# Gram products from two 64x64 tiles of the key tile instead of block-diagonal key copies

## The chip, the cores and the metric

The kernel runs on one core of one Trainium2 chip. The metric is the device time of one execution in microseconds. The core has a matrix engine (PE, with its weight loads PEld listed apart), a vector engine (DVE), a scalar engine (ACT), a general engine (POOL), and a queue engine (SP) that issues most DMAs. Each engine takes its instructions strictly in the order in which the built program holds them; an instruction that waits holds up all behind it on its engine.

## The reference

The kernel computes a delta-rule attention of 4 batches, 8 heads, 768 tokens and 48 features, and feeds its output, 3072 rows of 384, to a mixture of 8 experts with top-1 routing.

```python
k_n = k / (np.linalg.norm(k, axis=-1, keepdims=True) + 1e-06)
for t in range(S):
    y[:, :, t] = np.einsum('bhd,bhde->bhe', q[:, :, t], state)
    v_old = np.einsum('bhde,bhd->bhe', state, kt)
    state = state + bt[:, :, :, None] * np.einsum('bhd,bhe->bhde', kt, vt - v_old)
...
logits = x @ w_gate + modality_bias[modality_id]
e_idx = np.argmax(logits, axis=1)
h = np.maximum(x[mask] @ w1[e], 0.0)
out[mask] = gate_w[mask, None] * (h @ w2[e])
```

## The kernel before, in words

The recurrence is cut into 12 chunks of 64 tokens. A **group step** i = 2c+g is chunk c of one of two pairs of batches; there are 24. A step holds 16 heads, as 8 pairs x = 4p+j. Its key and query tile has 112 partitions: the 48 features of head 4h+j stand in rows 64h to 64h+47 (h = 0, 1), and for each x there are 64 key columns (a = 0) and 64 query columns (a = 1). For chunks 0 and 1 that tile is kqr, else ke, in five buffers; the load (L98, on SP) of ke i+5 waits until gram i has read its buffer.

`gram(i)` (L100) makes, for each x, the products of the step's keys with its keys and queries. The two heads of a pair must not mix. So it copies the keys into KB, a tile of 112 x 8 x 128 whose other blocks stay zero (cleared once, L85 and L86, one buffer on DVE and one on POOL): L111 to L113, one copy of 48x512 for each h, both on ACT for steps 0 to 3, one on ACT and one on DVE for 4 to 15, both on DVE from 16. Then L124 makes 8 products, 112x128 weights from KB by 128 moving columns, into two PSUM tiles gp (p = 0, 1). ACT and DVE copy the results out: G and gd (or D), the parts for the inverses (L126, L127), and P (L142, or L143 on DVE from step 16). From every second step of sets 2 to 5, G and gd go to DRAM by DMA (GD, L140).

An **inverse** (`inverse_`, L154) is made for each set of four steps, six sets m = 0 to 5. Its matrix A is a transposed copy of D for m = 0, 1 (L165, on DVE), and is loaded from GD by SP for the others (L166). ACT takes the root of its diagonal (s0, L175, named s01 for set 1, s02 for set 2), DVE goes on to t0 (t01, t02; L176 to L182) and scales A (L192), then DVE and POOL eliminate row by row (L213, L214: tm_x and T on DVE, tm_y and T on POOL). Set 0 is inverted in blocks of 16 and transposed to W0 (L225 to L228); `join` (L240) makes blocks of 32 from these: products jo on PE (L247), ya on DVE (L249), products on PE (L253), copies (R64, RTB). For set 1, D1's lower rows are filled late by ACT from PG (L150, "D<-PG"), behind the last copy of gram 13.

The **recurrence step** then runs: level products (L326, L335), the state's products ks (L363), RHS on DVE (L365), z (L378), ZT on ACT, the state's update (L386), the output y (L394), its store to xd, and the router's products for that step's 128 rows (L463, L468). After step 17 the first part of the routing and then the experts (L690, L733) start.

A scheduler with a timing model of its own sets the order on each engine when the program is built; a few gates (`issue_after`) bind single instructions to others. So a change of one part can move others.

Of the kernel before, what the change touches and what calls it, by code (L numbers as in the profile page):

```python
# [10 lines left out]
F32=mybir.dt.float32; F32R=mybir.dt.float32r; I32=mybir.dt.int32; U32=mybir.dt.uint32  # L11
# [3 lines left out]
class C:  # L15
    fl=4; mw=1; wn=2; kqb=5; kbb=2; thr=9; g0=17; nh=4; LA=2; LA0=1; ge=14; ge1=16; lgk={0:11,1:15,2:17,3:17}; gg={(12,0):('jy',0),(12,1):('jr',0),(13,0):('y1',0),(13,1):('r',0)}; ga=1; i1l=1; gdq=1;  gw=0; ww=512; t2e='vector'; dq1=('scalar','scalar'); jn={1:((1,0),)}; pf=0; gs=0
    invat={3:0,7:1,11:2,15:3,19:4,23:5}
    pgk=12; pgb=2; pgr=3; pg_q='sync'; gdb=2; kqr=2; kvb=2; r64=2; rtb=1; rcb=3; rbb=1; abuf=2; xob=2
    kb_q='sync'; gdfix='vector'; gdv=4; tmem='vector'; ascale='vector'; rscale='vector'; rcopy='mask'; rm_e='gpsimd'; vq='gpsimd'; yev='scalar'; sv=()
    x_q='sync'; xa_q='sync'; kv_q='sync'; ld_q='sync'; inv_q='sync'; w_q='sync'  # L20
    ap=(0,1); rp=(0,1); ra={0:('scalar','vector'),1:('scalar','vector')}; rs=(0,); i0=16; kb1=('scalar','vector'); g1=1; yq=2; na=1; xgb=4; wlp=('a1','b0'); wlq=(0,1,2,3); hpa=0; hpb=1; wide=1; zte=('scalar','scalar'); zti=4; pC_=None; pcn=(); gpt=('mo','ks','mo','y'); gpn=16; wte='vector'; ls=0; sp1=12; ti='gpsimd'; gde='scalar'; gde0='vector'; e16='scalar'; rh0='scalar'; as0='gpsimd'; dq=('vector','vector'); k1=1; rtg='gp'; rl=-1; fk=0; fz=0; fy=0; fi=0
    cA=9; tB=22; gt_e='gpsimd'; lb_e='vector'; TA=512; SB=1; SC=2; SE=1; eo=0; hold=1
# [3 lines left out]
    invp=(); kbc=24; dkb=0  # L26
    la_e='vector'; rw=dict(reuse_waits='tile'); pC=0; pI=None; pL=None; pin=(0,); pln=(0,); kbp=4; kbe0=('scalar','scalar'); kbe=('vector','vector'); pml=range(0,16); sp0=1; r0=6; NR=10; kg=0; a0=1; wr=4; gl=16; SA=4; i1=60

NS=16; NE=8

def copy(nc,n,o,i):
    if n=="scalar": nc.scalar.copy(o,i)  # L32
    else: getattr(nc,n).tensor_copy(o,i)
# [4 lines left out]
class Attention:  # L38
    """Chunked delta rule. Group step i=2c+g: 64 tokens of chunk c of batches 2g+p, heads 4h+j; x=4p+j."""
    def __init__(s,ident,ctx,pctx,tc,kq,kv,bblk,mask,xd,pm):  # L40
# [36 lines left out]
    def early(s,ctx):  # L77
        nc,tc=s.nc,s.tc
        s.pe=ctx[0].enter_context(s.tc.tile_pool(name="ag",bufs=1))
        s.pi=ctx[1].enter_context(s.tc.tile_pool(name="ai",bufs=1,side="right"))  # L80
        wt=s.wt=s.pe.tile([128,512],F32,name="wt")
        getattr(nc,C.wte).memset(wt,0.0)
        wz=s.pm.tile([128,512],F32,name="wz",tag="mo",bufs=2)
        for r in range(C.wn): nc.tensor.matmul(wz[:,0:C.ww],wt[:,0:128],wt[:,0:C.ww],start=True,stop=True)
        s.KB=[s.pe.tile([112,8,128],F32,name=f"KB{g}") for g in range(C.kbb)]  # L85
        for g,t in enumerate(s.KB): (s.nc.vector,s.nc.gpsimd)[g%2].memset(t,0.0)  # L86

# [12 lines left out]
    def gram(s,i):  # L100
# [8 lines left out]
        s.fetch(i)  # L109
        pg=s.PG[c]; k=s.KE[i]; KB=s.KB[i%C.kbb]  # L110
        for h in range(2):  # L111
            b=64*h
            copy(nc,(C.kbe0 if i<C.kbp else C.kb1 if i<C.i0 else C.kbe)[h],KB[b:b+48,:,b:b+64],k[b:b+48,:,0])  # L113
        s.Pt[i]=P=pg[:,512*g:512*g+512].rearrange("q (x t) -> q x t",x=8)
# [3 lines left out]
        for p in range(2):  # L118
          with s.gate(s.PI.get(C.gg.get((i,p)))):
            tg=C.gpt[(2*i+p)%len(C.gpt)] if i<C.gpn else "mo"  # L120
            gp.append((s.pm if tg=="mo" else s.ps).tile([128,4,128],F32,name=f"gp{i}_{p}",tag=tg,bufs=2 if tg=="mo" else None))
            for j in range(4):
                x=4*p+j
                nc.tensor.matmul(gp[p][:,j,:],KB[:,x,:],k[:,x].rearrange("r a t -> r (a t)"),start=True,stop=True)  # L124
        for p in range(2):
# [28 lines left out]
    def inverse_(s,m):  # L154
# [29 lines left out]
        def sub(X,a0,a1,b0,b1):  # L184
            """rows a0..a1, columns b0..b1 of the blocks on the diagonal"""
            return bass.AP(tensor=X.tensor,offset=X.offset+32*a0+b0,ap=[list(X.ap[0]),[33*B,nk],[32,a1-a0],[1,b1-b0]])
# [53 lines left out]
    def join(s,m,a,b):  # L240
        """blocks of 16 to blocks of 32 for columns a..b of W, D their Gram matrices"""
        nc=s.nc; N=b-a
        K=s.D[m].rearrange("q i x t -> q (i x) t")[:,a:b]; W0,W1=(t[:,a:b] for t in s.W[m])
        lv=s.ps.tile([128,512],F32,name=f"jo{a}",tag="gp")
        y,r=(lv[:,256*k:256*k+16*N].rearrange("q (n t) -> q n t",n=N) for k in range(2))
        for n in range(N):
            for q in range(0,128,32): s.PI['jy',a]=nc.tensor.matmul(y[q:q+32,n],K[q:q+16,n],W1[q:q+16,n,0:16],start=True,stop=True)  # L247
        ya=s.pw.tile([128,16,16],F32,name=f"ya{a}",tag="ya",bufs=1)
        s.PI['ya',a]=nc.vector.scalar_tensor_tensor(ya[:,0:N],y,s.m16,s.Ic.to_broadcast([128,N,16]),ALU.mult,ALU.add)  # L249
        if a==0 and C.gw:  # L250
            with s.gate(s.PI['ya',0]): s.w1b()
        for n in range(N):
            for q in range(0,128,32): s.PI['jr',a]=nc.tensor.matmul(r[q:q+32,n],W0[q:q+32,n],ya[q:q+32,n],start=True,stop=True)  # L253
        copy(nc,C.e16,W1[:,:,0:16],r)
        nc.vector.transpose(W0,W1)

    def joined(s,c,g):
        """inverse blocks of group g (or both) of a chunk of set 0"""
        if c not in s.KV: s.load(c)
# [143 lines left out]
def prep(q,k,v,beta):  # L403
    f=lambda a: a.reshape(2,2,2,4,12,64,48)  # g p h j c t e
    Q,K,V=f(q),f(k),f(v)
    kq=np.zeros((12,112,2048),np.float32); w=kq.reshape(12,112,2,2,4,2,64) # c r g p j a t
    for h in range(2):
        for a,X in enumerate((K,Q)): w[:,64*h:64*h+48,:,:,:,a]=X[:,:,h].transpose(3,5,0,1,2,4)
    kv=np.empty((12,2,64,2,2,2,4,48),np.float32) # c r t g a (two of p,h,j) e: keys with rows of a head, values with rows of a batch
    kv[:,:,:,:,0]=K.transpose(4,2,5,0,1,3,6)  # L410
    kv[:,:,:,:,1]=V.transpose(4,1,5,0,2,3,6)
    B=beta.reshape(2,2,2,4,6,2,2,32) # g p h j m cc b s
    bb=B.transpose(4,6,5,1,0,3,2,7).reshape(6,128,32).copy() # b cc p g j h
    for m in C.ap: bb[m]=B[:,:,:,:,m].transpose(2,5,4,0,1,3,6).reshape(128,32) # h b cc g p j
    t=np.arange(128)%64; mask=(t[:,None]<np.arange(64)[None,:]).astype(np.float32)
    return dict(kq=kq,kv=kv.reshape(12,128,1536),bblk=bb,mask=mask)
# [4 lines left out]
class Router:  # L421
    """Top-1 routing. Token tile i holds the rows of group step i. Tokens get places in lists of
    expert-pure slots: stages of whole 512-token slots first, the rest in 256-token slots."""
    def __init__(s,tc,pc,wg,mod,bias,ident):
# [45 lines left out]
    def rank(s,t0,t1,pw,ps,tag):  # L470
        """gates, experts, ranks among the tokens of an expert and one-hot ranks mod 128, of tiles t0..t1"""
        nc=s.nc; V=nc.vector; n=t1-t0; u=f"_{t0}"
# [37 lines left out]
    def stage(s,u,size,cap,col,pw):  # L510
        """share slots of size tokens out among the experts: slot experts, shift of the ranks"""
        nc=s.nc; V=nc.vector; m=s.edge[size].shape[1]
# [17 lines left out]
    def experts(s,u,hi,n,sei,pw):  # L530
        """expert of each slot, number of slots"""
        V=s.nc.vector
        T=lambda sh_,nm,dt=F32: pw.tile(sh_,dt,name=nm+u,tag=nm,bufs=1)
        cm=T([128,n,8],"cm"); V.tensor_tensor(cm,hi.unsqueeze(1).to_broadcast([128,n,8]),s.iot[:,0:n].unsqueeze(2).to_broadcast([128,n,8]),ALU.is_le)
        se=T([128,n],"se"); V.tensor_reduce(se,cm,AX.X,ALU.add)
        V.tensor_scalar(sei[:,0:n],se,7.0,None,ALU.min)
        V.tensor_copy(sei[:,n:n+1],hi[:,7:8])

    def look(s,u,t,Y,k,pw):
        """the values Y[k,expert] of the tokens' experts"""  # L540
        V=s.nc.vector; n=t//2
# [7 lines left out]
    def lists(s,u,t,pi,NH,out,pw,ps,tag,k):  # L549
        """place -> token and gate; NH columns of 128 places"""  # L550
        nc=s.nc; V=nc.vector; G=getattr(nc,C.lb_e)
# [71 lines left out]
class Experts:  # L623
# [10 lines left out]
    def weights(s,u,T,sei,col,gidx,c0,x,env,n=0):  # L634
        """weights and tokens of a slot"""
        nc=s.nc; E=getattr(nc,C.w_q)
# [63 lines left out]
    def layer1t(s,S):  # L700
        """layer 1 of 128 tokens: they are the rows of the products, which are transposed afterwards"""
        nc=s.nc; u=S["u"]; env=S["env"]; xh,xl=S["xh"],S["xl"]; W1,W2=S["W"][1],S["W"][2]
# [156 lines left out]
```

## Time and profile before

| | us |
|---|---|
| runs of the kernel | 552.22, 549.54, 549.57; median 549.57 |
| span of the profiled execution | 550.4 |
| PE busy | 483.5 (88%) |
| DVE busy | 364.5 (66%) |
| ACT busy | 263.5 (48%) |
| POOL busy | 208.5 (38%) |
| mean DMA rate over the span | 147 GB/s |

The times come from runs without the profiler; the profiled execution is one of its own, and its rows add up to its span. In the rows that follow, "out<-in" names the tiles with the buffer numbers left out, "xN" is a count, and a bracket at the end is the idle time just before, with what ended it. Weight loads (PEld) run beside products (PE). A PE row of a float32 product counts two records for each product in the program.

### The profile page before, as it was taken

The page shows a single profiled execution, that of the slowest core. Times are in us where ns is not written, and L with a number is a line of the kernel's source. Part 1 is how long each engine was busy: PE and PEld are TensorE (multiplying, and loading weights), DVE is VectorE, ACT ScalarE, POOL GpSimd, SP SyncE. Part 2 cuts the span into 40 slices and gives each one's busy share as a digit, 9 for nine tenths or more (in the row PEclk, how much of TensorE's full clock was granted, in tenths as well). Part 3 has the DMA queues.
Part 4 walks back from the last instruction along what each step waited for, and adds up shares of the span by engine and source line. Part 5 has one row for each costly group of instructions (what it writes and reads, how often), then busy time and mean ns, then how long its engine had stood idle before and what let it go on. Part 6 is the DMA issues. An engine that isn't in the chain of part 4 may idle for free. (4 is left out here: it accounts for less than half of the span.)

```text
span 550.4 us, 14025 instructions
## 1 busy us (share of the span) xinstructions
PE 483.5 (88%) x5459; PEld 432.1 (79%) x5459; DVE 364.5 (66%) x877; ACT 263.5 (48%) x619; POOL 208.5 (38%) x350
## 2 busy tenths in 40 slices
PE   7876875897898897998889997799999999999992
PEld 5776865786687776787768896689889898899992
DVE  5999899998789689577474499435536233437850
ACT  6855631655766567476565403043424334216540
POOL 9863477065066263111142136242303437111110
PEclk9977796588899799798889998699999999999997
DMA  8979741233594975838864224233623524427720
GB/s 205 247 200 238 176 105 55 64 95 89 169 226 138 236 180 166 209 120 230 228 192 142 76 80 127 75 116 114 209 79 120 170 75 164 128 78 227 233 85 9
DMA packets 82716, 80.81 MB, mean 147 GB/s; under 512 B 50105, under 2 KB 73671, under 8 KB 81520
## 3 DMA queue, kind: packets, MB, share of 16 engines
q1 hardware_dynamic: 79440, 70.18, 46.8%
q0 software_dynamic: 3200, 9.64, 5.2%
q8 instruction: 45, 0.74, 0.6%
q14 instruction: 31, 0.25, 0.2%
HBM read 65.12 MB, written 14.88 MB: 145 GB/s over the span
## 5 line engine op out<-in xcount | busy, mean ns | idle before, releaser
L733 PE MATMUL opa<-w2ha,h 128*128 128x384 f32 x256 | 69.1, 339 | 0.3 <-DVE ooa L736 0.3
L213 DVE TENSOR_TENSOR tm_x<-T,A 128x108 f32<-128x108 f32 (+12 forms) x165 | 57.8, 352 | 5.4 <-DVE PG L143 0.7
L124 PE MATMUL gp<-ke,KB 112*128 112x128 f32 x320 | 53.1, 331 | 9.3 <-DVE PG L143 3.9
L214 DVE TENSOR_TENSOR T<-T,tm_x 128x108 f32<-128x108 f32 (+12 forms) x165 | 56.8, 346 | 4.5
L124 PEld LDWEIGHTS gp<-ke,KB 112*128 112x128 f32 x320 | 48.3, 238 | 12.3 <-issue 3.7
L693 DVE SCALAR_TENSOR_TENSOR h<-hpa,h 128x512 fp32r<-128x512 f32 x32 | 22.0, 689 | 42.4 <-ACT h L692 42.4
L733 PEld LDWEIGHTS opa<-w2ha,h 128*128 128x128 f32 x256 | 46.2, 188 | 1.4 <-DVE ooa L736 0.5
L733 PE MATMUL opa<-w2la,h 128*128 128x384 f32 x128 | 43.0, 336 | 0.0
L692 ACT ACTIVATE h<-hpa 128x512 fp32r<-128x512 f32 x32 | 19.1, 596 | 49.5 <-PE hpa L690 49.5
L690 PE MATMUL hpa<-x,w1ha 128*128 128x512 f32 x144 | 39.1, 408 | 0.0
L340 POOL TENSOR_TENSOR kvn<-kvn,RR 128x384 f32<-128x384 f32 x22 | 18.7, 868 | 50.7 <-DMA kvn<-in_kv_dram 28.3
L363 PE MATMUL ks<-Sbd,kqr 112*64 112x96 f32 x352 | 27.3, 274 | 8.7 <-DMA kqr<-in_kq_dram 4.8
L365 DVE TENSOR_TENSOR RHS<-kvn,ks 64x384 f32<-64x384 f32 x44 | 24.2, 551 | 15.8 <-POOL kvn L340 9.4
L214 POOL TENSOR_TENSOR T<-T,tm_y 128x18 f32<-128x18 f32 (+8 forms) x90 | 30.7, 342 | 6.6
L213 POOL TENSOR_TENSOR tm_y<-T,A 128x18 f32<-128x18 f32 (+8 forms) x90 | 30.5, 339 | 6.6
L690 PEld LDWEIGHTS hpa<-x,w1ha 128*128 128x128 f32 x144 | 27.3, 194 | 5.5
L32 ACT COPY ZT<-z 64x384 f32<-64x384 f32 x48 | 22.7, 473 | 17.2 <-PE z L378 16.6
L363 PEld LDWEIGHTS ks<-Sbd,kqr 112*64 112x64 f32 x352 | 20.9, 150 | 11.8 <-ACT Sbd L32 4.4
L32 ACT COPY Sbd<-Sps 48x192 f32<-48x192 f32 x88 | 27.5, 313 | 5.2 <-PE Sps L386 2.7
L737 POOL DMA_INDIRECT out_dram<-ooa,sidxa x16 | 17.1, 1071 | 32.6 <-DMA out_dram<-ooa,sidxa 13.1
L657 POOL DMA_INDIRECT xga<-xd,gidxa x16 | 17.9, 1117 | 30.5 <-PE xpa L659 17.4
L378 PE MATMUL z<-RHS,R 128*64 128x96 f32 x384 | 26.9, 296 | 1.6 <-ACT R L338 1.6
(346 smaller groups left out, 1173.7 us busy)
## 6 DMA issues: line engine op xcount, KB each, us to landing
kvn<-in_kv_dram SPq DMA_DIRECT2D x12, 768.0 KB, 8.0
ke<-in_kq_dram SPq DMA_DIRECT2D x20, 448.0 KB, 6.8
kqr<-in_kq_dram SPq DMA_DIRECT2D x10, 896.0 KB, 6.9
w1ra<-in_moe_w_dram SPq DMA_DIRECT2D x16, 384.0 KB, 4.0
w2ra<-in_moe_w_dram SPq DMA_DIRECT2D x16, 384.0 KB, 3.2
xd<-xo SPq DMA_DIRECT2D x24, 192.0 KB, 2.5
w1rc<-in_moe_w_dram SPq DMA_DIRECT2D x8, 384.0 KB, 3.6
w2rc<-in_moe_w_dram SPq DMA_DIRECT2D x8, 384.0 KB, 3.2
```

What stands on the lines that cost most here:

```text
L32: if n=="scalar": nc.scalar.copy(o,i)
L124: nc.tensor.matmul(gp[p][:,j,:],KB[:,x,:],k[:,x].rearrange("r a t -> r (a t)"),start=True,stop=True)
L213: yield I.tensor_tensor(o,y,z,ALU.mult)
L214: yield I.tensor_tensor(x,x,o,ALU.subtract)
L340: if c: E(C.vq).tensor_tensor(V,V,w,ALU.mult)
L363: nc.tensor.matmul(ks[64*p:64*p+64,:,j,:],KQ[:,4*p+j,0],hc(Sb[:,4*p+j,:]),start=True,stop=True)
L365: b=64*p; nc.vector.tensor_tensor(RH[b:b+64,:,48*p:48*p+48].rearrange("q (h j) c -> q h j c",h=2),VN[b:b+64],ks[b:b+64],ALU.subtract)
L378: s.PI['z',i]=nc.tensor.matmul(z[64*h:64*h+64,:,j,:],R[:,2*j+h,:],hc(RH[:,4*h+j,:]),start=True,stop=True)
L690: nc.tensor.matmul(hp[:,v,:],w[:,k,fs],x[:,k,0:T],start=(n==0),stop=(n==8)); n+=1
L692: nc.scalar.activation(hh,hp,AF.Relu)
L693: nc.vector.scalar_tensor_tensor(hl,hp,0.0,hh.bitcast(F32),ALU.max,ALU.subtract)
L733: mm=nc.tensor.matmul(op,h[:,f%nf,ts_],w[:,f%2,:],start=(n==0),stop=(n==23)); n+=1
```

## The change

The copies into KB, the tiles KB, their clearing and the constants that chose their engines are gone. Each product of a pair becomes two, one for each head: weights are the 64 key columns of that head's 48 rows in the key tile, the moving columns the same rows' 128, and the result goes to 64 of the 128 rows of gp. What gp holds is the same. Comments and docstrings are removed as well, so lines stand 3 lower from L113 on (L247 is L244, L165 is L162, and so on) and 2 lower between L86 and L113.

```diff
-        s.KB=[s.pe.tile([112,8,128],F32,name=f"KB{g}") for g in range(C.kbb)]
-        for g,t in enumerate(s.KB): (s.nc.vector,s.nc.gpsimd)[g%2].memset(t,0.0)
...
-        pg=s.PG[c]; k=s.KE[i]; KB=s.KB[i%C.kbb]
-        for h in range(2):
-            b=64*h
-            copy(nc,(C.kbe0 if i<C.kbp else C.kb1 if i<C.i0 else C.kbe)[h],KB[b:b+48,:,b:b+64],k[b:b+48,:,0])
+        pg=s.PG[c]; k=s.KE[i]
...
-                nc.tensor.matmul(gp[p][:,j,:],KB[:,x,:],k[:,x].rearrange("r a t -> r (a t)"),start=True,stop=True)
+                for h in range(2):
+                    b=64*h
+                    nc.tensor.matmul(gp[p][b:b+64,j,:],k[b:b+48,x,0],k[b:b+48,x].rearrange("r a t -> r (a t)"),start=True,stop=True)
```

The built program's order differs at several places. On PE, these are the rows before around jo0, the products of set 0's join (W0_1, D0 and W0_0 are set 0's tiles, gpI_p the products of gram I; the number behind the last underscore is the program's own):

```order
L124 MATMUL gp8_1_469<-ke8_460,KB0_112 128x128 x4
L124 MATMUL gp9_0_486<-ke9_482,KB1_113 128x128 x4
...
L124 MATMUL gp13_1_592<-ke13_583,KB1_113 128x128 x4
L124 MATMUL gp14_0_1088<-ke14_1084,KB0_112 128x128 x4
L124 MATMUL gp14_1_1093<-ke14_1084,KB0_112 128x128 x4
L247 MATMUL jo0_619<-W0_1_283,D0_117 32x16 x32
L124 MATMUL gp15_0_1110<-ke15_1106,KB1_113 128x128 x4
```

and now:

```order
L121 MATMUL gp8_0_506<-ke8_504 64x128 x8
L121 MATMUL gp8_1_515<-ke8_504 64x128 x4
L244 MATMUL jo0_699<-W0_1_303,D0_113 32x16 x32
L121 MATMUL gp8_1_515<-ke8_504 64x128 x4
L121 MATMUL gp9_0_534<-ke9_532 64x128 x8
L121 MATMUL gp9_1_543<-ke9_532 64x128 x2
L250 MATMUL jo0_699<-ya0_732,W0_0_302 32x16 x32
L121 MATMUL gp9_1_543<-ke9_532 64x128 x6
```

The join moved from behind gram 14 to the middle of gram 8, so grams 9 to 14 stand behind it.

On ACT, these rows stood before around s02, the root that needs the loaded A2 (ZT0 is the copy of the recurrence's step 0, PG7 and gd7 are gram 15's results):

```order
L175 ACTIVATE s01_703<-A1_698,eps_96 128x32
L126 COPY PG7_1082<-gp15_1_1115 128x128
L32 COPY gd7_1083<-gp15_1_1115 128x128
...
L338 COPY R640_342<-y10_876 32x8x32 x2
L32 COPY ZT0_348<-z0_1306 64x8x48 x2
L175 ACTIVATE s02_913<-A2_908,eps_96 128x32
L126 COPY PG8_1341<-gp17_0_1739 128x128
```

and now:

```order
L139 COPY PG7_1162<-gp14_1_1175 128x256
L172 ACTIVATE s01_783<-A1_778,eps_96 128x32
L172 ACTIVATE s02_993<-A2_988,eps_96 128x32
L123 COPY PG7_1162<-gp15_0_1194 128x128
L32 COPY gd7_1163<-gp15_0_1194 128x128
...
L32 COPY ZT0_380<-z0_1398 64x8x48 x2
```

s02 moved ahead of gram 15's copies and of ZT0. On SP the load of A2 moved ahead of the load of ke19, which it followed.

On DVE, these rows stood before around t02, which needs s02 (tm1_x and T1 are set 1's elimination):

```order
L213 TENSOR_TENSOR tm1_x10_720<-T1_699,A1_698 128x30
L214 TENSOR_TENSOR T1_699<-T1_699,tm1_x10_720 128x30
L213 TENSOR_TENSOR tm1_x20_726<-T1_699,A1_698 128x58
L176 RECIPROCAL t02_914<-s02_913 128x32
L214 TENSOR_TENSOR T1_699<-T1_699,tm1_x20_726 128x2x29
L143 TENSOR_TENSOR PG8_1341<-gp17_0_1739,um_100 128x256
```

and now:

```order
L162 STREAM_TRANSPOSE A1_778<-D1_308 128x1024
L173 RECIPROCAL t01_784<-s01_783 128x32
L174 TENSOR_TENSOR t01_784<-t01_784,A1_778 128x32
L175 TENSOR_TENSOR t01_784<-t01_784,s01_783 128x32
L173 RECIPROCAL t02_994<-s02_993 128x32
L176 TENSOR_SCALAR rr1_786<-t01_784 128x32
...
L189 TENSOR_TENSOR A1_778<-A1_778,t11_785 128x1024
```

t02 moved ahead of set 1's scaling and elimination. Further on, the inverses of sets 2 to 5 stand earlier among the recurrence's steps on DVE: of the 330 elimination instructions, 173 stood ahead of the RHS of step 8, and 270 stand there now.

More of the change, by code (lines that the diff above doesn't have):

```diff
@@ L15 @@
 class C:
-    fl=4; mw=1; wn=2; kqb=5; kbb=2; thr=9; g0=17; nh=4; LA=2; LA0=1; ge=14; ge1=16; lgk={0:11,1:15,2:17,3:17}; gg={(12,0):('jy',0),(12,1):('jr',0),(13,0):('y1',0),(13,1):('r',0)}; ga=1; i1l=1; gdq=1;  gw=0; ww=512; t2e='vector'; dq1=('scalar','scalar'); jn={1:((1,0),)}; pf=0; gs=0
+    fl=4; mw=1; wn=2; kqb=5; thr=9; g0=17; nh=4; LA=2; LA0=1; ge=14; ge1=16; lgk={0:11,1:15,2:17,3:17}; gg={(12,0):('jy',0),(12,1):('jr',0),(13,0):('y1',0),(13,1):('r',0)}; ga=1; i1l=1; gdq=1;  gw=0; ww=512; t2e='vector'; dq1=('scalar','scalar'); jn={1:((1,0),)}; pf=0; gs=0
     invat={3:0,7:1,11:2,15:3,19:4,23:5}
@@ L20 @@
     x_q='sync'; xa_q='sync'; kv_q='sync'; ld_q='sync'; inv_q='sync'; w_q='sync'
-    ap=(0,1); rp=(0,1); ra={0:('scalar','vector'),1:('scalar','vector')}; rs=(0,); i0=16; kb1=('scalar','vector'); g1=1; yq=2; na=1; xgb=4; wlp=('a1','b0'); wlq=(0,1,2,3); hpa=0; hpb=1; wide=1; zte=('scalar','scalar'); zti=4; pC_=None; pcn=(); gpt=('mo','ks','mo','y'); gpn=16; wte='vector'; ls=0; sp1=12; ti='gpsimd'; gde='scalar'; gde0='vector'; e16='scalar'; rh0='scalar'; as0='gpsimd'; dq=('vector','vector'); k1=1; rtg='gp'; rl=-1; fk=0; fz=0; fy=0; fi=0
+    ap=(0,1); rp=(0,1); ra={0:('scalar','vector'),1:('scalar','vector')}; rs=(0,); i0=16; g1=1; yq=2; na=1; xgb=4; wlp=('a1','b0'); wlq=(0,1,2,3); hpa=0; hpb=1; wide=1; zte=('scalar','scalar'); zti=4; pC_=None; pcn=(); gpt=('mo','ks','mo','y'); gpn=16; wte='vector'; ls=0; sp1=12; ti='gpsimd'; gde='scalar'; gde0='vector'; e16='scalar'; rh0='scalar'; as0='gpsimd'; dq=('vector','vector'); k1=1; rtg='gp'; rl=-1; fk=0; fz=0; fy=0; fi=0
     cA=9; tB=22; gt_e='gpsimd'; lb_e='vector'; TA=512; SB=1; SC=2; SE=1; eo=0; hold=1
@@ L26 @@
     invp=(); kbc=24; dkb=0
-    la_e='vector'; rw=dict(reuse_waits='tile'); pC=0; pI=None; pL=None; pin=(0,); pln=(0,); kbp=4; kbe0=('scalar','scalar'); kbe=('vector','vector'); pml=range(0,16); sp0=1; r0=6; NR=10; kg=0; a0=1; wr=4; gl=16; SA=4; i1=60
+    la_e='vector'; rw=dict(reuse_waits='tile'); pC=0; pI=None; pL=None; pin=(0,); pln=(0,); pml=range(0,16); sp0=1; r0=6; NR=10; kg=0; a0=1; wr=4; gl=16; SA=4; i1=60
 NS=16; NE=8
```

## The prediction

> **What bounds the kernel now.** First the page's 40 slices (13.76 us each, tenths of busy time), then stretches of 20 and 50 us with each engine's busy time.
>
> ```profile
> PE   7876875897898897998889997799999999999992
> DVE  5999899998789689577474499435536233437850
> DMA  8979741233594975838864224233623524427720
> ```
>
> ```profile
> 20.00:40.00 20.00, 16.23 (x119) 15.73 (x120) 18.89 (x35) 13.24 (x51) 15.96 (x23) 0.83 0.88 219
> 40.00:60.00 20.00, 14.76 (x211) 13.53 (x209) 19.14 (x38) 11.89 (x42) 7.23 (x11) 0.74 0.98 245
> ```
>
> ```profile
> 350.00:400.00 50.00, 50.00 (x245) 44.53 (x245) 21.05 (x38) 17.12 (x27) 13.88 (x12) 0.94 0.41 127
> 400.00:450.00 50.00, 49.75 (x254) 44.80 (x254) 20.20 (x30) 18.11 (x30) 13.37 (x11) 1.00 0.36 112
> ```
>
> The columns are the stretch, its length, busy PE, PEld, DVE, ACT and POOL, the PE clock, the DMA share and GB/s. The experts at the end are PE's alone (50.00 of 50). From 20 to 60 us DVE is the full engine (18.89 and 19.14 of 20), and so, over 40 to 60, are the DMA engines (0.98). So what changes in the expert stage is nothing, and the question is when the recurrence delivers its tokens. Steps 8 and 17 of it measure that.
>
> ```profile
> 164.16 0.55 PE L463 MATMUL rxt<-ident,xo 128*128 128x128 f32 x3
> 164.63 0.88 PE L378 MATMUL z<-RHS,R 128*64 128x96 f32 x16
> ...
> 170.66 0.55 PE L463 MATMUL rxt<-ident,xo 128*128 128x128 f32 x3
> ```
>
> ```profile
> 237.96 0.88 PE L378 MATMUL z<-RHS,R 128*64 128x96 f32 x16
> ```
>
> Columns: start, duration, line, tiles, count. Step 8's z starts at 164.63, step 17's at 237.96, after which the router and the first experts can start. A step in which PE runs back to back takes 6.50 us (164.16 to 170.66). Nine steps took 73.33, where nine of 6.50 are 58.5: 14.8 us went into waits for later inverses and loads. I take a shift of step 17 as a shift of the end, since the PE-bound experts follow it.
>
> **The change, part by part.** *The products themselves.* A step's 8 products of 112x128 weights become 16 of 48x64.
>
> ```profile
> L124 PE MATMUL gp<-ke,KB 112*128 112x128 f32 x320 | 53.1, 331 | 9.3 <-DVE PG L143 3.9 <-issue 2.7 <-ACT s L175 1.1
> L33 DVE COPY KB<-ke 48x512 f32<-48x512 f32 x28 | 15.5, 553 | 0.8 <-PE gp L124 0.3
> L32 ACT COPY KB<-ke 48x512 f32<-48x512 f32 x12 | 7.5, 621 | 0.2
> L32 ACT COPY KB<-kqr 48x512 f32<-48x512 f32 x8 | 4.9, 617 | 3.1 <-DVE Ic L62 2.7 <-DMA kqr<-in_kq_dram 0.3
> ```
>
> ```profile
> 38.28 2.02 PE L124 MATMUL gp<-ke,KB 112*128 112x128 f32 x16 [0.19 <-ACT PG L142]
> 41.05 2.02 PE L124 MATMUL gp<-ke,KB 112*128 112x128 f32 x16 [0.75 <-ACT PG L142]
> ...
> 49.28 1.05 PE L247 MATMUL jo<-W,D 16*32 16x16 f32 x64 [3.55 <-DVE W L225]
> ...
> 60.56 0.69 PE L335 MATMUL y<-R,ys 32*32 32x32 f32 x32 [0.86 <-ACT ys L330]
> ```
>
> Each product leaves two records, so a step has 16 in 2.02 us, or 126 ns for 128 columns. The new step has 32 records; the moving columns stay 128. If the two tiles of a head pair run beside each other, a step stays near 2.02; if they queue, it takes 32 x 126 ns = 4.03. No row shows 64x64 tiles on a diagonal. The nearest is L335, 32x32 tiles on several rows: 32 records of 32 columns in 0.69, where 126 ns scaled to 32 columns (31.5 ns) would queue to 1.01. They overlap, so I take 2.02, with 4.03 as the other end. The Trainium skill's "TensorEngine Tiling (Array Packing)", Gotcha 1, speaks against this: different row tiles cannot use one PSUM bank at the same time, and here both tiles write halves of one gp tile. By that rule the step would take the 4.03 us; the L335 row, whose tiles also share a bank, does not bear it out. That is rival C.
>
> *The copies.* Gone are 28 on DVE (15.5 us), 20 on ACT (12.4) and a clearing each on DVE and POOL. On DVE this lies in its full stretch, so taken alone it is time on the path. Twelve of the 28 stand in the order ahead of W's first transpose (L225), which ends set 0's inverse.
>
> ```profile
> 48.19 1.03 DVE L225 STREAM_TRANSPOSE W<-T 128x512 f32<-128x512 f32 x1
> ...
> 52.98 1.91 DVE L165 STREAM_TRANSPOSE A<-D 128x1024 f32<-128x1024 f32 x1
> ```
>
> ```profile
> L86 DVE MEMSET KB<- x1: 912/912/912, 2.7 to 2.7; 112x1024 f32 x1
> ```
>
> It ends at 49.22; less 12 x 0.553 and the 0.91 clearing, at about **41.7**. Nothing else ahead of it changes.
>
> *What the order makes of it.* On PE the products of the join, jo0 on W0, move from behind gram 14 into the middle of gram 8. PE is in order, so grams 8 to 15 now wait for 41.7, although gram 9 to 13 need only their keys; before, grams 10 and 11 ran at 38.28 and 41.05. A step comes every 2.77 us there (41.05 - 38.28); without the 0.62 us copy on ACT perhaps every 2.15. I take 2.4: gram 11, 3.5 steps after the join's first half, is done at 50.1; gram 13, 5.5 steps after it, at 54.9. Two things hang on that. ACT's late copies of D1 follow gram 13:
>
> ```profile
> 43.85 3.30 ACT L32 COPY D<-PG 32x256 f32<-32x256 f32 x8
> ```
>
> so D1 is whole at 54.9 + 3.3 = 58.2 instead of 47.15, and DVE's transpose of A1 behind it ends at 60.1 instead of 54.9. And the key loads: with five buffers, ke16 waits for gram 11, ke18 for gram 13, and the load of A2 stands on SP behind them.
>
> ```profile
> 38.16 0.32 SPq L98 DMA_DIRECT2D ke<-in_kq_dram  x1
> ...
> 45.24 0.43 SPq L296 DMA_DIRECT2D kqr<-in_kq_dram  x1
> ...
> 50.09 3.86 SPq L98 DMA_DIRECT2D ke<-in_kq_dram  x1
> 54.05 0.38 SPq L166 DMA_DIRECT2D A<-GD x1
> ```
>
> ```profile
> 39.70:54.40 14.70, 9.77 (x150) 9.00 (x152) 14.16 (x24) 8.80 (x31) 6.21 (x9) 0.83 0.98 250
> ```
>
> ```profile
> DMA to landing us min/median/max: 3.2/5.0/6.8
> ```
>
> Before, ke16 was issued at 38.16 and the queue came to 50.09, 11.9 us later, before the wait for ke19's buffer, which A2 now precedes. The DMA engines moved 250 GB/s at a share of 0.98 meanwhile, so the backlog sets this pace. From 50.1: A2 issued at 62.0 and, with the longest landing of A's loads (the last row, 6.8), landed at **68.8**. The ends: 54.9 + 2 for the writes of GD3 + 3.2 gives 60.1; the whole stretch of 14.7 started only at ke18's issue, and a median landing of 5.0 behind it, give 75.
>
> *What waits for A2.* Now ACT has s02, the root of A2's diagonal, ahead of gram 15's copies and of ZT0, without which no recurrence step ends; and DVE has t02 ahead of the whole elimination of A1, where before t02 stood behind its first two columns. So DVE stands from A1's transpose until A2 has landed, and cannot use that time for A1's elimination.
>
> *What DVE does afterwards.* Counting in the order: between t02 and the RHS of step 8 there were 141 elimination instructions (L213, L214) and are now 241, for sets 3 and 4 stand ahead of it; ten KB copies there are gone.
>
> ```profile
> 64.51 0.35 DVE L176 RECIPROCAL t<-s 128x32 f32<-128x32 f32 x1 [0.42 <-ACT s L175]
> ...
> 163.67 1.12 DVE L365 TENSOR_TENSOR RHS<-kvn,ks 64x384 f32<-64x384 f32 x2
> ```
>
> ```profile
> 64.00:165.00 101.00, 83.80 (x1575) 72.93 (x1576) 89.41 (x251) 53.04 (x151) 50.03 (x132) 0.82 0.43 112
> ```
>
> ```profile
> 64.00:165.00 101.00, 26.37 (x77) 0.82 0.43 112
> ```
>
> ```profile
> L192 DVE TENSOR_TENSOR A<-A,t x5: 1208/1218/1226, 60.8 to 183.2; 128x1024 f32<-128x1024 f32 x5
> ```
>
> The stretch from t02 to step 8 lasted 99.2 us with 89.4 busy. One elimination instruction takes 0.342 (the row with 26.37 is L213 alone, x77). New busy time: 89.4 + 100 x 0.342 - 10 x 0.553 + about 6 for the added sets' scalings (five as L192 at 1.22) = 124.1. Of the 9.8 idle I keep 4, since DVE now comes last more often. RHS of step 8: 69.3 (A2's 68.8 and the root) + 128.1 = **197.4**, its z 1 us later. In return all inverses are done early, and steps 8 to 17 can run at PE's 6.50: step 17's z at 198.4 + 58.5 = **256.9**, against 237.96: +18.9. Short: z17 = t02 + 187.6. The removal of the copies is in this sum; the reordering outweighs it.
>
> **Against the runs.** The profiled execution spans 550.4, the median of the runs is 549.57. 550.4 + 18.9 = 569.3 in the profile; 0.8 off for the runs, and 1.5 off because the wait of step 19 for its inverse goes as well: **567**.
>
> **Rivals.** A, *A2 is not late* (no change): the stall needs the DMA backlog. If grams 9 to 13 follow one another at 2.02 and A2 lands as soon as issued, t02 is not at 69 but near 52. By z17 = t02 + 187.6, no change is at t02 = 50.4; DVE's own work would let it reach t02 there (64.51 less 12 + 6 copies at 0.553 and the clearing is 53.6, and the first columns of A1 moved behind it). For: SP issues A2 one load earlier. Against: D1's copies alone hold A1 until 58.2. 549 to 553.
>
> B, *faster*: as A, and in addition the eliminations speed up, for one shape has two prices.
>
> ```profile
> 31.42 0.79 DVE L213 TENSOR_TENSOR tm_x<-T,A 128x110 f32<-128x110 f32 x1
> ...
> 40.98 0.27 DVE L213 TENSOR_TENSOR tm_x<-T,A 128x110 f32<-128x110 f32 x1
> ```
>
> If the mean of 0.342 fell to 0.29 with less beside them, 241 x 0.05 = 12 us would go: 537 to 546. It decides where t02 comes before 60. Against it: POOL's own eliminations, which run beside DVE's, stay.
>
> C, *the tiles queue*: 2.0 us more for each gram step. Steps 9 to 13 are ahead of A2: +10 on t02 at most, and steps 16 to 23 add PE time where it waits for DVE: 575 to 585.
>
> D, *that the copies' removal does nothing* (DVE hidden behind DMA) falls into A's times.
>
> **How the numbers follow.** Forecast (t02 60 to 75, z17 +9.6 to +24.6): 0.60; C 0.12; A and D 0.13; B 0.15. "Within 0.5%", about what a measurement of this kernel can tell from no change, is 2.7 us. Faster 0.15, same 0.13, slower 0.72. The forecast's own range is 557 to 573 and a little beyond for the idle kept (up to 5.8 more: 579). For 8 in 10 the range goes to 546 below, which takes in A, and to 581, part of C.
>
> **What would show it.** PE's idle time before L244 rises from 3.55 us to over 10 and ends on DVE's W. L121's steps of 32 records take near 2.0 us at full clock (4 would be C). A2's load is issued near 62, ACT's s02 waits for it, and DVE idles some 8 us or more before t02. Step 8's z lies near 198 and step 17's near 257, with 6.5 us between steps. The prediction is wrong if DVE does not idle before t02, or if the steps before 8 wait less for DVE than 124 us of work says.

## The result and the profile after

The changed kernel takes 586.45 us (583.08 to 587.92), the kernel before 549.57; the ratio is 1.0655, 95% interval 1.0607 to 1.0703. The profiled execution spans 586.1 us against 550.4. It is slower, as forecast, but by 36.9 us instead of 17.4, and outside the range (546 to 581).

The page's slices of the changed kernel, then its group of Gram products (count, busy us, mean ns of one, idle time before, and what ended it):

```profile
PE   8629567766849789899998999689999999999992
DVE  4981199999998569611378348934455423546750
PEclk9855865557856969999998899859999999999998
...
L121 PE MATMUL gp<-ke 48*64 48x128 f32 x640 | 61.5, 351 | 20.5 <-DVE PG L140 12.8
```

A slice is 14.65 us here. DVE is nearly idle in the fourth and fifth (44 to 73 us), where it had been full, and then full to about 190. The products of the 20 ke steps are busy for 61.5 us, where L124 had 53.1, and they wait 12.8 us for DVE's copies of P (L140), where it was 3.9. The rise in busy time isn't the price of the tiles: in e10 below, the same 640 records take 51.4.

The rows around the first inverse, PE's first, then SP's, then DVE's; a bracket is the idle time before a row:

```profile
40.08 1.05 PE L244 MATMUL jo<-W,D 16*32 16x16 f32 x64 [12.92 <-DVE W L222]
...
50.24 3.68 PE L121 MATMUL gp<-ke 48*64 48x128 f32 x32
```

```profile
65.91 3.91 SPq L163 DMA_DIRECT2D A<-GD  x1
```

```profile
65.10 1.95 DVE L162 STREAM_TRANSPOSE A<-D 128x1024 f32<-128x1024 f32 x1 [17.70 <-ACT D L32]
73.40 0.35 DVE L173 RECIPROCAL t<-s 128x32 f32<-128x32 f32 x1 [5.11 <-ACT s L172]
205.54 0.35 DVE L173 RECIPROCAL t<-s 128x32 f32<-128x32 f32 x1 [6.34 <-ACT s L172]
```

PE stands 12.92 us for W in the middle of gram 8. DVE then stands 17.70 us for D1's late copies and 5.11 for the root that needs A2. The third row is not in the prediction: at 205.54 DVE stands again, for set 5's root. Steps 8 and 17 of the recurrence, PE's row of z, and DVE's stretch that the prediction summed, from t02 to the RHS row that starts just ahead of step 8's z (216.71):

```profile
217.73 0.88 PE L375 MATMUL z<-RHS,R 128*64 128x96 f32 x16
```

```profile
278.82 0.88 PE L375 MATMUL z<-RHS,R 128*64 128x96 f32 x16
```

```profile
73.40:216.71 143.31, 102.80 (x1685) 87.59 (x1687) 122.46 (x352) 59.41 (x163) 66.54 (x168) 0.65 0.39 105
```

Step 17 comes 40.9 us later than before (237.96), the end 35.7. The stretch is 143.3 us with 122.5 busy on DVE, where it was 99.2 with 88.0 busy. (The prediction's 89.4 is of the 101 us from 64 to 165.)

One reading of the prediction has to be put right here. The row that it calls the RHS of step 8 (163.67 before) is that of step 9: steps 0 and 1 have no such row, and the one with 173 eliminations ahead of it, which is the count given for step 8, stands at 158.01. In the change the row with 270 ahead of it stands at 208.06, and 216.71 is step 9's. From t02 to step 8's own RHS the two kernels have, before first:

```profile
64.51:158.01 93.50, 76.53 (x1432) 66.52 (x1433) 82.83 (x235) 47.88 (x137) 43.78 (x115) 0.81 0.39 105
```

```profile
73.40:208.05 134.65, 95.22 (x1575) 80.91 (x1577) 118.29 (x338) 53.83 (x151) 61.55 (x156) 0.65 0.37 100
```

DVE is busy 118.3 us instead of 82.8, and idle 16.4 instead of 10.7. So the finding is the same by either row: the loss is mostly DVE's work, moved ahead of step 8.

### The profile page after: what moved, and what is told of

Read it like the earlier page. It is cut to its first block, busy times and chain, and to the rows that moved or that the text cites. A ratio compares the mean times of both kernels' runs of the same rounds, so it can differ in the third digit from the quotient of the medians.

```text
span 586.1 us, 14707 instructions
## 1 busy us (share of the span) xinstructions
PE 495.7 (85%) x5843; PEld 441.3 (75%) x5843; DVE 350.0 (60%) x848; ACT 253.0 (43%) x599; POOL 206.2 (35%) x349
## 4 chain that ended last, share of the span: by engine, by line
PE 56%; DVE 27%; DMA 6%; issue 4%; ACT 3%; SPq 1%; POOL 0%; POOLq 0%; ACTq 0%; DVEq 0%
PE hpa L687 12%; PE opa L730 10%; DVE T L211 7%; DVE tm_x L210 7%; PE gp L121 4%; PE hpc L687 3%; PE opc L730 3%; PE opb L730 3%; PE hpb L687 2%; PE Sps L465 2%; DMA A<-GD 2%; PE y L391 2%; PE Sps L383 2%; PE z L375 2%; DVE RHS L362 1%
## 5 line engine op out<-in xcount | busy, mean ns | idle before, releaser
L121 PE MATMUL gp<-ke 48*64 48x128 f32 x640 | 61.5, 351 | 20.5 <-DVE PG L140 12.8
L121 PEld LDWEIGHTS gp<-ke 48*64 48x64 f32 x640 | 52.8, 181 | 24.8 <-DVE PG L140 14.7
L210 DVE TENSOR_TENSOR tm_x<-T,A 128x108 f32<-128x108 f32 (+12 forms) x165 | 57.8, 352 | 6.1 <-issue 1.3
L211 DVE TENSOR_TENSOR T<-T,tm_x 128x108 f32<-128x108 f32 (+12 forms) x165 | 55.9, 340 | 4.9
L211 POOL TENSOR_TENSOR T<-T,tm_y 128x18 f32<-128x18 f32 (+8 forms) x90 | 32.2, 359 | 6.6
L123 ACT COPY PG<-gp 128x128 f32<-128x128 f32 x48 | 12.9, 268 | 44.2 <-PE gp L121 43.9
L210 POOL TENSOR_TENSOR tm_y<-T,A 128x18 f32<-128x18 f32 (+8 forms) x90 | 29.0, 323 | 6.8
L142 POOL TENSOR_SCALAR_AFFINE_SELECT PG<-PG 64x512 f32<-64x512 f32 x32 | 21.9, 686 | 16.0 <-ACT PG L139 14.7
L465 PE MATMUL Sps<-wg,rxs 128*128 128x96 f32 x144 | 25.0, 318 | 3.0 <-ACT rxs L462 3.0
```

The source lines that it names most:

```text
L121: nc.tensor.matmul(gp[p][b:b+64,j,:],k[b:b+48,x,0],k[b:b+48,x].rearrange("r a t -> r (a t)"),start=True,stop=True)
L142: for h in range(2): nc.gpsimd.affine_select(out=P[64*h:64*h+64],in_=P[64*h:64*h+64],compare_op=ALU.is_gt,fill=0.0,base=0,pattern=[[0,8],[ ...
L210: yield I.tensor_tensor(o,y,z,ALU.mult)
L211: yield I.tensor_tensor(x,x,o,ALU.subtract)
L465: for k in range(3): nc.tensor.matmul(s.lg[g][:,c0:c1,:],xs[:,k,:],s.wg[:,k,88-8*(c-c0):88+8*(c1-c)].rearrange("q (c e) -> q c e",e=8),sta ...
```

## The experiments

"Eliminations" are DVE's instructions of L213 and L214 (L210 and L211 in the change). Times of t02 and z are the starts in the profiled execution; the count ahead, of the RHS of steps 2 and 8, is that of the built order. Each ratio is to the kernel before, run on the same chip; the medians of different runs can be from different chips.

| run | join | ahead of step 2, 8 | t02 | z8 | z17 | median | ratio |
|---|---|---|---|---|---|---|---|
| before | behind gram 14 | 41, 173 | 64.5 | 164.6 | 238.0 | 549.57 | 1 |
| change | in gram 8 | 62, 270 | 73.4 | 217.7 | 278.8 | 586.45 | 1.0655 |
| e1 | in gram 8 | 59, 270 | 84.5 | 230.2 | 291.5 | 598.01 | 1.0842 |
| e2 | behind gram 13 | 83, 270 | 56.1 | 208.9 | 271.3 | 577.94 | 1.0478 |
| e3 | in gram 9 | 30, 174 | 77.2 | 174.2 | 247.1 | 554.28 | 1.0054 |
| e4 | behind gram 13 | 90, 196 | 84.7 | 181.0 | 253.9 | 559.98 | 1.0123 |
| e5 | in gram 8 | 62, 270 | 83.6 | 211.4 | 272.9 | 579.41 | 1.0528 |
| e6 | late | 66, 287 | 64.3 | 207.1 | 278.4 | 590.23 | 1.0725 |
| e7 | late | 41, 172 | 65.7 | 159.8 | 230.7 | 548.18 | 0.9971 |
| e8 | late | 46, 175 | 72.1 | 167.0 | 238.0 | 555.46 | 1.0110 |
| e9 | in gram 8 | 62, 270 | 73.7 | 207.5 | 270.0 | 581.92 | 1.0553 |
| e10 | behind gram 13 | 30, 192 | 68.8 | 160.2 | 230.5 | 542.40 | 0.9850 |
| e11 | late | 30, 172 | 73.1 | 165.2 | 239.1 | 548.55 | 0.9989 |
| e12 | as e10 | 30, 192 | 67.8 | 161.0 | 231.1 | 543.34 | 0.9908 |

**e1, the products alone.** Two-tile products in the kernel before, whose copies stay:

```diff
-                nc.tensor.matmul(gp[p][:,j,:],KB[:,x,:],k[:,x].rearrange("r a t -> r (a t)"),start=True,stop=True)
+                for h in range(2):
+                    b=64*h
+                    nc.tensor.matmul(gp[p][b:b+64,j,:],k[b:b+48,x,0],k[b:b+48,x].rearrange("r a t -> r (a t)"),start=True,stop=True)
```

> The products in two tiles as in the change, but the block-diagonal copies and their clearing stay (nothing reads them). In the built order the join stands in gram 8 here too. Theory O (the loss comes from the order that 16 products a step bring about, and the copies' removal is worth some us): 588 to 604, as the change and with the copies' time on top. Rival R (it is the removal of the copies that shifts the order and costs the time): 549 to 556. Rival P (the two-tile products are themselves dearer on the chip): 586 or above too, but with gram steps well over 2.0 us at full clock.

598.01 us (interval of the ratio 1.0748 to 1.0936), with the join in gram 8 and 270 eliminations ahead of step 8. The new order comes with the products' count, not with the copies' removal; in nearly the same order (59 and 62 eliminations ahead of step 2) the copies cost 11.6 us more (598.01 against 586.45, two different chips).

**e2, the join held back.** One gate in the change:

```diff
-            for q in range(0,128,32): s.PI['jy',a]=nc.tensor.matmul(y[q:q+32,n],K[q:q+16,n],W1[q:q+16,n,0:16],start=True,stop=True)
+            for q in range(0,128,32):
+                with s.gate(s.PI['g'] if a==0 else None): s.PI['jy',a]=nc.tensor.matmul(y[q:q+32,n],K[q:q+16,n],W1[q:q+16,n,0:16],start=True,stop=True)
```

where 'g' is the latest Gram product, that of gram 13.

> The change, with the first products of set 0's join held behind gram 13 on PE; the rest of the order stays as the change has it (270 eliminations ahead of step 8). Theory O: gram 13 is done near 43 instead of 60.6 us, A2 lands near 59, t02 starts near 60 instead of 73.4, and the end moves by as much: 568 to 578. Rival P: 583 or above. Rival D (all of the loss is in the order of the eliminations on DVE, the join's place costs nothing): 583 or above.

577.94 (1.0387 to 1.0569). PE's row of grams 7 to 11 and DVE's t02:

```profile
23.71 8.77 PE L121 MATMUL gp<-ke 48*64 48x128 f32 x150
```

```profile
56.12 0.35 DVE L173 RECIPROCAL t<-s 128x32 f32<-128x32 f32 x1 [7.80 <-ACT s L172]
```

150 records in 8.77 us are 58.5 ns each, 1.87 us for a step's 32, against 2.02 before. In the trace they start in pairs, 6 or 7 ns apart, with a new pair every 109 ns: the tiles do run beside each other, and rival C falls. The median is at the end of theory O's 568 to 578. t02 came 17.3 us earlier than in the change, but step 8 only 8.8 and the median 8.5: half of an early t02 is lost behind it, where the eliminations stand as in the change. Part of it goes where DVE waits for the root of set 5, 10.4 us here:

```profile
198.57 0.35 DVE L173 RECIPROCAL t<-s 128x32 f32<-128x32 f32 x1 [10.38 <-ACT s L172]
```

**e3, the join early in the kernel before.** It is emitted after gram 8, with a gate that is to hold gram 9 behind it:

```diff
-gg={(12,0):('jy',0),(12,1):('jr',0),(13,0):('y1',0),(13,1):('r',0)}
+gg={(9,0):('jy',0),(9,1):('jr',0)}
...
         i=nxt; G1(i); nxt+=1
+        if i==8:
+            with tc.high_priority(): A.joined(0,0)
```

> The kernel before (wide products, copies kept), with the join emitted after gram 8 and grams 9 to 13 held behind it on PE, so the join's place is the change's and 174 eliminations stand ahead of step 8 (173 before). Theory O: PE stands until W is there (near 49 us), gram 13 is done near 63, t02 starts near 76 instead of 64.5, and the end comes 6 to 14 us later: 556 to 564. Rival D: 549 to 553. Rival R or P (the join's place is not what costs): 549 to 553 as well.

554.28 (1.0015 to 1.0093), under the 556 to 564 of theory O and above its rivals' 553.

```profile
42.44 1.05 PE L247 MATMUL jo<-W,D 16*32 16x16 f32 x64 [6.22 <-DVE W L225]
```

In the trace the first half of gram 9 ran ahead of the join, and PE stood 6.22 us for W, not the change's 12.92, so e3 is a weaker form of the change's stall. t02 is 12.7 us later than before, step 17 9.2 and the span 7.2 in the profiled execution, which was the slowest of the eight (559.35); the median is 3.4 later. A part of a late t02 is made good where the eliminations stand as before. How large a part, these runs don't settle.

**e4, the sets spread.** e2, and the inverses of sets 2 to 5 are emitted after steps 2, 4, 7 and 11:

```diff
-        V.reciprocal(t0,s0)
+        with s.gate(s.PI['rh',{2: 2, 3: 4, 4: 7, 5: 11}[m]] if m in {2: 2, 3: 4, 4: 7, 5: 11} else None): V.reciprocal(t0,s0)
...
         A.chain(i)
+        for m in {2: (2,), 4: (3,), 7: (4,), 11: (5,)}.get(i,()): A.inverse(m)
```

'rh',i is the RHS of step i on DVE.

> The change, with the join held behind gram 13 and the inverses of sets 2 to 5 emitted later, their t0 held behind the RHS of steps 2, 4, 7 and 11 on DVE: 196 eliminations ahead of step 8 instead of 270. Theory O: both losses go and the copies' 16 us of DVE stay away: 543 to 556. Rival P: 570 or above, since every gram step is as in the change. Rival J (only the join's place costs, the order of the eliminations does not): as e2, 568 to 578.

559.98 (1.0052 to 1.0195): 18 us below e2, but 4 above what theory O expected. Step 2's z started at 123.9 us here and at 108.8 before: 90 eliminations, the 30 of set 0 and all 60 of set 1, were ahead of its RHS, where it had been 41. e10 takes that up.

**e5, the roots behind.** In the change, sets 2 and 3 are emitted after step 0, and two gates set:

```diff
+        with s.gate(s.PI['zt'] if m==2 else None): nc.scalar.activation(s0,d,AF.Sqrt,bias=s.eps)
+        with s.gate(s.PI['el'] if m==2 else None): V.reciprocal(t0,s0)
```

> The change, with the inverses of sets 2 and 3 emitted after step 0, s02 held behind ZT0 on ACT and t02 behind the 24th elimination instruction of set 1 on DVE; the join stays in gram 8. Theory O: the 5.1 us that DVE stood before t02 and the 5.6 us of ACT before s02 go, the later waits stay: 579 to 584. Rival W (the order of the roots is a large part of the loss): below 575. Rival N (A2's wait is hidden, only its volume of work counts): 585 to 588.

579.41 in two runs (575.87 and 582.95); the median is at the lower end of theory O's 579 to 584, and the two runs lie on either side of it. Undoing the wait for A2's root, the stall that the prediction put first, brings 3 to 11 us of the 37.

**e6, the eliminations' order alone.** Two-tile products from step 16 on only:

```diff
-        for h in range(2):
+        for h in range(0 if i>=16 else 2):
             b=64*h
             copy(nc,(C.kbe0 if i<C.kbp else C.kb1 if i<C.i0 else C.kbe)[h],KB[b:b+48,:,b:b+64],k[b:b+48,:,0])
...
+                if i>=16:
+                    for h in range(2):
...
+                else: nc.tensor.matmul(gp[p][:,j,:],KB[:,x,:],k[:,x].rearrange("r a t -> r (a t)"),start=True,stop=True)
```

> Wide products with copies for steps 0 to 15, two-tile products without copies from step 16 on. In the built order the join stays late (behind gram 13), but 287 eliminations stand ahead of step 8 instead of 173. It tries the order of the eliminations alone. Theory O: t02 near 62 to 65 as before, z of step 8 near 185 to 195 instead of 164.6, and the end 10 to 22 us above before: 560 to 572. Rival J (only the join's place costs): 540 to 550, since 16 of DVE's copies are gone.

590.23 (1.0625 to 1.0825), as slow as the change and far above both theories' numbers. t02, DVE's stretch from 64 to 207 us, and step 8:

```profile
64.29 0.34 DVE L180 RECIPROCAL t<-s 128x32 f32<-128x32 f32 x1
```

```profile
64.00:207.00 143.00, 97.19 (x1676) 81.91 (x1672) 122.53 (x354) 56.85 (x151) 65.94 (x172) 0.69 0.37 101
```

```profile
207.06 1.55 PE L382 MATMUL z<-RHS,R 128*64 128x96 f32 x16
```

The join is late, t02 stands where it stood before (64.51), 16 copies are gone from DVE, and the kernel is 40 us slower. From t02 to step 8's z it is 142.8 us, in the change 144.3, and before 100.1. So most of the loss lies in what stands between t02 and step 8. The number of eliminations there stands for the whole of the inverses that moved: their roots on ACT, their loads on SP and POOL's share moved with them, and no run moves the one without the other.

**e7, narrow from step 20.** e6 with 20 for 16, and with it an order like that of before.

> Wide products with copies for steps 0 to 19, two-tile products without copies for steps 20 to 23; the order is nearly that of before (172 eliminations ahead of step 8, join behind gram 14). Eight copies of 0.55 us leave DVE. Theory O: 544 to 550. Rival P (a gram step in two tiles is dearer on the chip): 552 or above.

548.18 (0.9932 to 1.0010): as expected, though no difference from before that the interval settles.

**e8, narrow up to step 3.** e6's edit with the condition i<4.

> Two-tile products without copies for steps 0 to 3, wide ones with copies from step 4; 175 eliminations ahead of step 8, the join behind gram 12. Eight copies of 0.62 us leave ACT in the first 13 us, where gram 0 waits for its copy. Theory O: set 0's inverse starts 1 to 2.5 us earlier and the end follows or stays: 545 to 551. Rival P: 552 or above.

555.46 (1.0022 to 1.0197), where theory O expected 545 to 551; the number is rival P's. PE's rows of the first steps:

```profile
6.31 4.07 PE L127 MATMUL gp<-kqr 48*64 48x128 f32 x64
14.14 1.97 PE L127 MATMUL gp<-kqr 48*64 48x128 f32 x16 [3.76 <-ACT PG L146]
```

Two steps take 4.07, so it isn't the rate; the wait of 3.76 for ACT's copies in the third step is new. I expected an earlier inverse and overlooked what else ACT's queue holds there. It is a KB copy of a later step, which waited 4.92 us for its load with the copies of PG behind it:

```profile
12.99 0.62 ACT L32 COPY KB<-ke 48x512 f32<-48x512 f32 x1 [4.92 <-DMA ke<-in_kq_dram]
13.71 0.37 ACT L146 COPY PG<-gp 128x256 f32<-128x256 f32 x1
```

How the rest of the 5 us follows was not tried.

**e9, set 5 later.** In the change, set 5 alone is emitted after step 9, its root and t05 behind that step's ZT and RHS:

```diff
+        with s.gate(s.PI['zt',{5: 9}[m]] if m in {5: 9} else None): nc.scalar.activation(s0,d,AF.Sqrt,bias=s.eps)
+        with s.gate(s.PI['rh',{5: 9}[m]] if m in {5: 9} else None): V.reciprocal(t0,s0)
...
+        for m in {9: (5,)}.get(i,()): A.inverse(m)
```

> The change, with only set 5's inverse emitted later: after step 9, its root s05 behind ZT of step 9 on ACT and its t05 behind the RHS of step 9 on DVE; everything up to step 6 as the change has it. The change's trace shows PE 5.0 us and DVE 6.3 us idle at step 7, ended by the root of set 5, whose matrix A5 had not landed. Theory S (that wait is a wait of its own on the path): step 8's z 5 to 10 us earlier than the change's 217.7 and the end with it, 574 to 582. Rival H (the time comes back at once, because DVE's eliminations are due anyway): step 17's z within 3 us of 278.5 and the end 584 to 588.

581.92 in two runs (579.22 and 584.62); in the profiled execution step 8 stands 10.2 us earlier than in the change, step 17 8.9, and the span is 577.5. The trace speaks for theory S: that wait was on the path by itself. The times alone don't settle it, since the slower of the two runs lies within the change's 583.08 to 587.92.

**e10, the sets spread from the first.** e4, with sets 1 and 2 emitted after step 2, set 1's eliminations held behind its RHS, and the roots behind the ZT of steps 0, 3, 6 and 10:

```diff
-                x=next(g,None)
+                with s.gate(s.PI['rh',{1: 2}[m]] if m in {1: 2} and g is st[0] else None): x=next(g,None)
...
+        for m in {2: (1, 2), 4: (3,), 7: (4,), 11: (5,)}.get(i,()): A.inverse(m)
```

> The change, with the join held behind gram 13, sets 1 and 2 emitted after step 2 and set 1's eliminations held behind the RHS of step 2 (30 eliminations ahead of it), sets 3 to 5 behind the RHS of steps 4, 7 and 11, and every root behind a ZT; 192 eliminations ahead of step 8. It is e4 with the early steps freed as well. Theory O (the place of the eliminations between the steps is the main cost): steps 2 and 3 at 100 to 118 as before and not at 125 to 138, the end 540 to 553. Rival P (with every product in two tiles something else keeps at least 10 us): 558 or above.

542.40 us, 0.985 (0.9777 to 0.9922): faster than both kernels, with every product in two tiles and no copy. Step 2's z starts at 108.2 us, as it did before. Step 8's z, and DVE from 64 to 165 us, where it is busy for 92.1 (89.4 before):

```profile
160.20 0.88 PE L375 MATMUL z<-RHS,R 128*64 128x96 f32 x16
```

```profile
64.00:165.00 101.00, 85.88 (x1688) 73.76 (x1688) 92.12 (x271) 53.15 (x147) 42.74 (x112) 0.76 0.47 123
```

**e11 and e12, the control.** The kernel before with e10's holds, and e10 again beside it.

> The kernel before (wide products, copies kept) with the same holds as e10: 172 eliminations ahead of step 8, 30 ahead of step 2. It asks how much of e10's gain over the kernel before is in the holds and how much in the missing copies. Theory O (in a like order the missing copies are worth something, since DVE is full until step 8): 546 to 553, at least 4 us above e12. Rival G (the gain of e10 is all in the holds): 539 to 545, within 2 us of e12.

> The same kernel as e10, run beside e11 on one chip. Theory O: 540 to 545 and at least 4 us below e11. Rival G: within 2 us of e11.

e11: 548.55 (0.9958 to 1.0019). e12: 543.34 (0.9879 to 0.9938). The holds by themselves bring nothing that can be measured; with them, the products without copies bring 5.2 us against e11. The two orders are close, not the same (192 and 172 eliminations ahead of step 8), so the 5.2 us is the worth of the change in a like order, not the copies' alone.

## Why the prediction was wrong in size

*The direction and its cause were right:* the order, not the products, makes it slower (e6, e7, e10). The rows asked for came in part: 12.92 us of PE idle ahead of the join, and idle DVE ahead of t02, though only 5.11 us of it directly ahead and 17.70 ahead of A1's transpose.

*The products* were taken at 2.02 us a step, which e2 shows at 1.87. The rule of the Trainium skill's "TensorEngine Tiling (Array Packing)", Gotcha 1, would have made it about 4 by the prediction's estimate. The measurement decides against it: no run shows 4 at full clock.

*W and t02.* The join was expected at 41.7 and came at 40.08. t02 was expected at 69.3 and came at 73.40: 4.1 of the error. The low clock was not in the sum: after PE's idle time a gram step took 3.68 us (row 50.24), not 2.4, and the last record of gram 13 started at 60.6, where the sum had the gram done at 54.9.

*The step that failed* is the stretch behind t02, "Of the 9.8 idle I keep 4, since DVE now comes last more often". DVE's busy time was about right, 122.5 against 124.1, though the sum took 100 added eliminations for a stretch whose rows have 93 more (244 against 151). Its idle time was 20.8 instead of 4: 143.3 us in place of 128.1, 15.2 of the error. The 9.8 was too small to begin with (89.4 busy us of a longer window, taken from 99.2); it was 11.1. What ended DVE's idle time in the change between 64 and 217 us (us in total, times, longest), where the first row and 5.5 us of the second lie ahead of t02:

```profile
DVE A L162 <- ACT D L32: 17.7, 1, 17.7
DVE t L173 <- ACT s L172: 12.1, 4, 6.3
DVE RHS L362 <- PE ks L360: 3.7, 3, 2.9
DVE tm_x L210 <- issue: 1.3, 1, 1.3
```

Of the roots' 12.1 us, 6.34 are set 5's, at 205.54. I had looked at s02's place in ACT's queue, and not at s05's, which had also moved ahead of step 7's copies:

```profile
206.19 0.90 PE L460 MATMUL rxt<-ident,xo 128*128 128x128 f32 x3 [5.02 <-ACT R L335]
```

PE waits there for a copy that stands behind that root. A5's load was issued at 200.15, when the results of gram 23, the last, had been written. Gram 23 ran from 176.9 to 188.0 us, before from 130.1 to 135.0, and DVE's copies of its P stand behind 236 and 241 of the 330 eliminations, before behind 129 and 134. Ahead of it, grams 17, 18, 20 and 22 had waited for such copies (the 12.8 us in L121's group). So work brought forward, the root, waited for work that had been pushed back; which of these waits makes how much of gram 23's delay was not tried.

The wait has a second price. From step 7's z to step 8's PE has nearly the same records in both kernels, but after the 5.02 us it runs at a mean granted clock of 0.60 (the column after the engines), before at 1.00, and takes 10.71 us instead of 6.81:

```profile
157.82:164.63 6.81, 6.58 (x138) 5.71 (x137) 6.14 (x15) 4.52 (x12) 5.79 (x17) 1.00 0.89 213
```

```profile
207.02:217.73 10.71, 9.63 (x139) 8.45 (x138) 6.18 (x17) 6.32 (x13) 6.81 (x17) 0.60 0.76 210
```

Step 8's own RHS was done at 209.2, so here it is PE that step 8's z waits for, and DVE's 2.88 us for L360 is a wait for PE as well: the prediction's path from DVE's work straight to that z does not hold. e9 takes set 5's wait away and gains 10.2 us at step 8. Some 8 us more of the idle are the gaps of mostly 20 to 40 ns between 352 instructions, as between these two:

```profile
197.13 0.22 DVE L210 TENSOR_TENSOR tm_x<-T,A 128x60 f32<-128x60 f32 x1
197.39 0.22 DVE L211 TENSOR_TENSOR T<-T,tm_x 128x60 f32<-128x60 f32 x1
```

Such gaps made 4.9 us before, with 248 instructions, and they grow with the count.

*The formula z17 = t02 + 187.6* gave t02 too much weight. By it e6 would have had step 17 at 251.9 and e2 at 243.7; they had 278.4 and 271.3. The order behind t02 carries the larger part: e6 alone is 40 us above before with t02 unmoved, while the join's place costs 8.5 us in the change's order (e2) and, in its weaker form, some 3 in that of before (e3).

*The recovery* was taken at 58.5 us for nine steps and was 61.1 (278.82 - 217.73): 2.6. At the end 5.2 us of step 17's delay did not arrive, 1.5 were expected. Together: 4.1 + 15.2 + 2.6 is 21.9 at step 17, less 3.7 at the end; the measured error there is 18.3 in the profile (35.7 against 17.4).

*Rivals.* A and B needed t02 below 60 without cost behind it; e2 had t02 at 56.1 and was 4.8% slower. D has no support: in a like order the missing copies are worth some 5 us (e12 against e11).

What stays open: why the scheduler's timing model moves the eliminations ahead when the products double in number was not looked into, only that it does (e1, e6); whether the inverses' eliminations, roots or loads count for more in it, beyond set 5's root (e9); and of e8's 5 us only the first wait is shown.

## What to carry to other kernels

Where a scheduler sets the order from its own timing, a change that doubles the number of instructions can move everything around them: compare the order of each engine first, and read a loss there before blaming the instructions. On a full engine, count what stands ahead of the step that others wait for, and follow every load that the moved work needs, not the first alone. An edit that loses by its order can be worth keeping: here three kinds of holds turned 6.6% slower into 0.9 to 1.5% faster.

## What the runs showed of the hardware

Two 64x64 tiles on the array's diagonal, writing two halves of the same PSUM tile, ran beside each other: 58.5 ns a record of 128 columns where a single 112x128 tile took 126. After 12.92 us of idle PE the clock stayed low for a long time, though PE was busy throughout: the changed kernel had a mean granted clock of 0.50 (the column after the engines) for 18 us, from 40 to 58, and 0.95 in the 6 us behind.

```profile
40.00:58.00 18.00, 17.92 (x300) 16.62 (x302) 4.47 (x10) 8.30 (x31) 3.92 (x6) 0.50 0.53 143
58.00:64.00 6.00, 6.00 (x108) 6.00 (x106) 0.00 (x0) 5.02 (x18) 5.50 (x8) 0.95 0.95 214
```

Behind the 5.02 us of idle PE at 201 to 206 it was low again, 0.60 over the 10.71 us from step 7 to step 8. What ends such a stretch, no run here was made to show.
